# Attention and the layers behind it in one hand-ordered region: the drain of attention, the first in-blocks and their banks

## The chip, the cores and the metric

The kernel runs on one core of one Trainium2 chip. What is measured is the device time of one execution in microseconds (us). A core has TensorE (PE, matmuls, whose weight loads the profile lists as PEld), VectorE (DVE), ScalarE (ACT), GpSimd (POOL) and SyncE (SP, which issues most of the transfers). Each engine runs its own list of instructions in order and waits on semaphores for the others. PSUM, into which PE writes, has eight banks.

## What is computed

Windowed attention with four sink keys over q, k, v of shape (2, 8, 768, 64), then two feed-forward layers of 512 to 2048 to 512 over the 1536 tokens:

```python
scores = scale * np.matmul(q, k.transpose(0, 1, 3, 2))
keep = is_sink | in_window                      # 4 sinks, window of 128
scores = np.where(keep, scores, -1000000000.0)
a = np.exp(scores - max); a = a / (sum + 1e-09)
x = np.matmul(a, v)                             # to (1536, 512)
h = np.maximum(x @ w_in, 0.0);  x = h * h @ w_out            # layer 1
h = x @ w_in2; g = h * np.tanh(log1p(exp(h))); out = g @ w_out2   # layer 2
```

## The kernel before

**Attention** works on 12 tiles of 128 query rows and in each on 4 pairs of heads, 48 pairs in all. A loop over pair steps n (from -3 to 52) is software-pipelined: at step n it issues the scores of pair n+4 (`emit_s`, tile `s`), the exp of pair n+3 (`emit_exp`, on ScalarE), the normalization of pairs n+2, n+3 (`emit_norm`, on POOL, at even n), the transposes of pairs n-1, n (`emit_t`, tile `pt`, at odd n), their copies to SBUF (`evac_t`, tile `pts`, on ScalarE or DVE) and the products with v of pairs n-4, n-3 (`emit_av`, tile `av`, at even n). When a tile of rows is done, `emit_x` copies it out (`xf`, on ScalarE), casts it to a rounded part `xh` (POOL) and subtracts to get the rest `xl`: on POOL for the first ten tiles, and for tiles 10 and 11 on DVE, one or more steps later (`split_x`). Once the scores run out, at step 44, the last steps are the drain. PSUM is split into four banks for `s`, three for `pt` and one for `av`, in this order.

**A layer** works on 3 groups of 512 tokens (`xh[0]` to `xh[2]`; tiles 8 to 11 are group 2) and on 16 blocks of 128 hidden units. A sub-step n is one group and one block: an in-block of 12 matmuls into a bank `h`, then relu, square and a cast to `gh` on ScalarE (`relu_squared`), a subtraction to `gl` on DVE (`low_part`), and one sub-step later the out-block: 12 matmuls into four accumulators `o`, in the order gh·wol, gl·woh, gh·woh for each. PSUM has four banks for `h` and four for `o`.

**Weights** come as 64-bit words (tile `raw`, three slots) and each block's two halves, wi and wo, are converted by a `Conv`: a scaled copy of the high words (`head`, ScalarE), two DVE instructions on the bits (`mid_r`, lines 136 and 142), one that joins them (`mid_or`, line 148), the rounded part on ScalarE (`high`: wih or woh, line 167) and the rest on DVE (`low`: wil or wol, line 171). Three of them (`blocks` 0 to 2: block 0's wi and wo, block 1's wi) are done during attention, at the pair steps that the table `PLAN` gives; the function `slot` does the others in layer 1, two to each sub-step, those that `done_w` doesn't name, in the order wi(2), wo(1), wi(3), wo(2) and on. `IN_AT` gives the pair steps at which attention issues the in-blocks of sub-steps 0 and 1; they lie in banks of `s`, and their relu and gl follow one and two steps later.

The loop over pairs and the layers stand in two regions (`tc.manual_schedule()`), each with the order of its code. Across the two, the built program has the layers' first conversions in between the drain's last instructions.

Of the kernel before, what the change touches and what calls it, by code (L numbers as in the profile page):

```python
# [9 lines left out]
F32 = mybir.dt.float32  # L10
# [5 lines left out]
ALU = mybir.AluOpType  # L16
PSUM = bass.MemoryType.PSUM
P = 128
# [5 lines left out]
def f32(ap):  # L24
    return ap.bitcast(F32)
# [3 lines left out]
def kernel(  # L29
# [13 lines left out]
    nc = tc.nc  # L43
# [3 lines left out]
    NB = S // P  # L47
    NPAIR = H // 2
# [143 lines left out]
    def in_products(ph, w, sp):  # L192
        for m, (a, x) in enumerate([("wil", xh[sp]), ("wih", xl[sp]), ("wih", xh[sp])]):
            for d in range(NDC):
                nc.tensor.matmul(  # L195
                    ph, lhsT=w[a][:, d, :], rhs=x[:, d, :],
                    start=(m == 0 and d == 0), stop=(m == 2 and d == NDC - 1),
                )

    def new_g(pool):  # L200
        return [pool.tile([P, TS], F32R, tag=nm, name=nm, bufs=2) for nm in ("gh", "gl")]

    def relu_squared(ph, gh):
        nc.scalar.activation(out=ph, in_=ph, func=AF.Relu)  # L204
        nc.scalar.activation(out=ph, in_=ph, func=AF.Square)
        nc.scalar.copy(gh, ph)  # L206

    def low_part(x, gh, gl):
        nc.vector.tensor_tensor(out=gl, in0=x, in1=f32(gh), op=ALU.subtract)  # L209


    att = ExitStack()
    apool = att.enter_context(tc.tile_pool(name="apool", bufs=1))
    ps_s = att.enter_context(tc.tile_pool(name="ps_s", bufs=4, space=PSUM, reuse_waits="tile"))
    ps_p = att.enter_context(tc.tile_pool(name="ps_p", bufs=3, space=PSUM, reuse_waits="tile"))
    ps_a = att.enter_context(tc.tile_pool(name="ps_a", bufs=1, space=PSUM, reuse_waits="tile"))

    tiles = [(b, i) for b in range(B) for i in range(NB)]
    qn, kn, vn = {}, {}, {}
# [100 lines left out]
    def prep(t, which, half=None):  # L320
        if t >= len(tiles):
            return
        b, i = tiles[t]
        js = slice(0, NPAIR) if half is None else slice(half * NPAIR // 2, (half + 1) * NPAIR // 2)
        src = (qn if which == "q" else kn)[b, i]
        pt = ps_p.tile([P, NPAIR, P], F32, tag="pt", name="tr")
        for j in range(js.start, js.stop):
            nc.tensor.transpose(  # L328
                pt[:, j, :], src[:, 2 * j : 2 * j + 2, :].rearrange("p h d -> p (h d)"), ident
            )  # L330
        if which == "q":
            nc.vector.tensor_copy(kt[:, js, qpos(t) : qpos(t) + P], pt[:, js])
        else:
            p0 = kpos(i)
            nc.scalar.copy(kt[:, js, p0 : p0 + P], pt[:, js])
# [164 lines left out]
    def emit_x(b, i):  # L500
        hi, lo = x_slot(b, i)
        x = apool.tile([P, NPAIR, P], F32, tag="xf", name="xf", bufs=1)
        nc.scalar.copy(x, av.pop((b, i)))
        nc.gpsimd.tensor_copy(hi, x)
        if b * NB + i < len(tiles) - 2:
            nc.gpsimd.tensor_tensor(out=lo, in0=x, in1=f32(hi), op=ALU.subtract)
        else:
            st["x"] = (x, hi, lo)

    def split_x():  # L510
        if "x" in st:
            x, hi, lo = st.pop("x")
            nc.vector.tensor_tensor(out=lo, in0=x, in1=f32(hi), op=ALU.subtract)

    blocks = []
    for fb in range(W1N):
        wt[0, fb] = weight_tiles(w1pool, fb)
        blocks += [Conv(conv, 0, fb, part, wt[0, fb]) for part in ("wi", "wo")]
    WARM = (6, 3, 2, 1)
    PLAN = {  # L520
        0: {5: "load", 11: "head", 14: "mid_r1", 18: "mid_r2", 22: "mid_or", 26: "high low"},
        2: {36: "load", 41: "head_pool", 44: "mid_r", 45: "mid_or", 46: "high low"},
        1: {37: "load", 46: "head mid_r", 47: "mid_or", 48: "high low"},
    }

    IN_AT = (46, 48)
    SINKS = {n0 + 2 * (i - 2): i for n0 in (-1, NB * NPAIR - 3) for i in range(2, NB)}
    early, ready = {}, {}
    NPR = len(pairs)
    with tc.manual_schedule():  # L530
        load_limits()
        nc.scalar.preload_act_table_set("natural_log_exp_and_others")
        load_tile(0, "qk", halves=2)
        load_tile(1, "qk")
        load_tile(2, "kq")
        load_tile(0, "v")
        load_tile(3, "kq")
        positions()
        load_tile(1, "v")
        load_tile(2, "v")  # L540
        load_rest(2)
        warm = apool.tile([P, P], F32, name="warm")
        nc.vector.memset(warm, 0.0)
        nc.vector.memset(one, 1.0)
        nc.gpsimd.memset(two, 2.0)
        for x in prs:
            nc.gpsimd.memset(x[:, :, WIN:], 0.0)
        for x in sums:
            nc.vector.memset(x, 1e-9)
        idle = ps_a.tile([P, P + 2], F32, tag="av", name="idle")  # L550

        def keep_warm(times):
            for _ in range(times):
                nc.tensor.matmul(idle[:, 0:P], lhsT=warm, rhs=warm, start=True, stop=True)  # L554

        keep_warm(WARM[0])
        limits(idle[:, P : P + 2])
        first_mask()
        prep(0, "q", 0)
        keep_warm(WARM[1])  # L560
        prep(0, "k", 0)
        keep_warm(WARM[2])
        emit_s(*pairs[0])
        emit_max(*pairs[0], 0)
        emit_max(*pairs[0], 1)
        prep(0, "q", 1)
        prep(0, "k", 1)
        emit_s(*pairs[1])
        emit_max(*pairs[1], 0)
        emit_max(*pairs[1], 1)  # L570
        second_mask()
        window_masks()
        emit_exp(*pairs[0])
        for n in range(-3, NPR + 5):
            at = {d: pairs[n + d] for d in range(-4, 5) if 0 <= n + d < NPR}
            last = {d for d in at if at[d][2] == NPAIR - 1}
            t, j = divmod(n, NPAIR)
            if n % 2 and 0 in at:
                emit_t([at[-1], at[0]])
            if 4 in at and n > -3:  # L580
                emit_s(*at[4])
            if 3 in at and n > -3:
                emit_exp(*at[3])
            if 4 in at and n > -3:
                emit_max(*at[4], 0)
            if 4 in at and n > -3:
                emit_max(*at[4], 1)
            if n % 2 == 0:
                split_x()
                group = [at[d] for d in (2, 3) if d in at]  # L590
                if group:
                    emit_rs(group)
                for p in group:
                    emit_norm(*p)
            if -4 in last:
                emit_x(*at[-4][:2])

            if n % 2 == 0:
                if n >= 0 and j == 2:
                    prep_rows(t + 2)  # L600
                for d in (-4, -3):
                    if d in at:
                        emit_av(*at[d])
            for _ in range((1, 2, 0, 1)[j]):
                evac_t()
            if n in (-3, -2):
                prep(1, "qk"[n + 3])
            if n >= 0 and j == NPAIR - 1:
                load_tile(t + 4, "q", halves=1 + (t + 5 == len(tiles)))
                load_tile(t + 4, "k", halves=1 + (t + 6 >= len(tiles)))  # L610
                load_tile(t + 3, "v")
                load_rest(t + 3)
            if n in SINKS:
                sink_keys(SINKS[n])
            if n < 0:
                keep_warm(WARM[3])
            if n == 1:
                fast_flag()
            for fb in range(W1N):
                if n == IN_AT[fb]:  # L620
                    early[fb] = ps_s.tile([P, TS], F32, tag="s", name="h")
                    in_products(early[fb], wt[0, fb], 0)
                if n == IN_AT[fb] + 1:
                    ready[fb] = new_g(gpool)
                    relu_squared(early[fb], ready[fb][0])
                if n == IN_AT[fb] + 2:
                    low_part(early[fb], *ready[fb])
            for m, steps in PLAN.items():
                for step in steps.get(n, "").split():
                    getattr(blocks[m], step)()  # L630
    att.close()


# [261 lines left out]
    ps_o = mo.enter_context(tc.tile_pool(name="ps_o", bufs=4, space=PSUM, reuse_waits="tile"))  # L895
    engines = [getattr(mybir.EngineType, e) for e in ("PE", "DVE", "Activation", "Pool", "SP")]
    tc.mark_branch_hint_location("general", hint="LikelyTaken", engines=engines)
    with tc.manual_schedule():
        moe(
            wt, lambda fb: w1pool if fb < W1N else w2pool, conv, gpool, ps_h, ps_o,  # L900
            done_in=ready, done_w=[(0, blocks[m].fb, blocks[m].part) for m in PLAN],
        )
    mo.close()
    main.close()

# [141 lines left out]
```

## Time and profile before

| | |
|---|---|
| median of 3 runs | 614.54 us (614.17 to 614.92) |
| the profiled execution | 614.09 us, of which the trace's span is 612.3 us |
| PE, DVE, ScalarE, POOL busy | 98%, 74%, 57%, 12% of the span |
| matmuls of the layers start | 79.79 us (h of sub-step 0), 90.24 us (first out-block) |
| last matmul ends | 607.35 us |

A timeline row gives the start in us, the duration, the engine, the line, the operation with the tiles written and read, and the count; at its end may stand the idle time before it and what ended that. A row's duration includes the engine's latency, so back-to-back instructions start closer together than their durations say. Attention's drain is at 76 to 90 us; the conversions of layer 1's weights run on DVE and ScalarE until about 160 us.

### The profile page before, as it was taken

The numbers are of one execution on the slowest core, as the hardware profiler recorded it, in microseconds if no ns is written. First come the engines' busy times: TensorE is split into PE (matmuls) and PEld (weight loads), VectorE is DVE, ScalarE is ACT, GpSimd is POOL, SyncE is SP. The second block draws the span as 40 slices with busy tenths as digits, with TensorE's granted clock in tenths as the row PEclk, the third lists the DMA queues.
The fourth block names the chain that finished last, engine by engine and source line by source line (L and its number), as shares of the span: only waits on it lengthen the run. The fifth ranks groups of instructions, "written<-read, shape, count | busy, mean of one in ns | idle before, by whom it ended". The sixth has DMA issues, their size and how long they took to land.

```text
span 612.3 us, 10256 instructions
## 1 busy us (share of the span) xinstructions
PE 602.5 (98%) x3854; PEld 493.7 (81%) x3854; DVE 452.9 (74%) x951; ACT 349.6 (57%) x723; POOL 70.6 (12%) x103
## 2 busy tenths in 40 slices
PE   9999989999999999999999999999999999999996
PEld 6786778888888888888888888888888888888885
DVE  5898889989621111188889699999888778887784
ACT  4999976777643333277777555555454444544442
POOL 5889940000000000000000000000000000000000
PEclk9999999999999999999999999999999999999999
DMA  9989746666400000036666300000010000100001
GB/s 190 191 179 185 195 139 179 202 204 196 148 1 0 2 0 1 0 113 197 205 190 193 101 1 2 0 1 1 1 69 1 0 1 0 44 27 1 0 1 71
DMA packets 71704, 49.45 MB, mean 81 GB/s; under 512 B 49508, under 2 KB 66148, under 8 KB 71652
## 3 DMA queue, kind: packets, MB, share of 16 engines
q1 hardware_dynamic: 71360, 48.38, 29.1%
q8 instruction: 31, 0.51, 0.3%
q10 hardware_dynamic: 292, 0.39, 0.2%
q14 instruction: 21, 0.17, 0.1%
HBM read 45.61 MB, written 3.15 MB: 80 GB/s over the span
## 4 chain that ended last, share of the span: by engine, by line
PE 94%; DVE 2%; POOL 1%; ACT 1%; issue 1%; DVEq 0%; ACTq 0%; POOLq 0%
PE o L658 43%; PE h L195 42%; PE s L398 3%; PE av L488 3%; PE pt L451 2%; PE idle L554 1%; PE tr L346 1%; POOL pr L439 1%; DVE cv_r L142 0%; PE tr L328 0%; ACT pr L419 0%; DVE cv_a L148 0%; DVE pts L466 0%; DVE s L409 0%; DVE cv_r L136 0%
## 5 line engine op out<-in xcount | busy, mean ns | idle before, releaser
L195 PE MATMUL h<-xh,wil 128*128 128x512 f32 x384 | 102.9, 390 | 0.0
L195 PE MATMUL h<-xl,wih 128*128 128x512 f32 x384 | 102.6, 389 | 0.0
L195 PE MATMUL h<-xh,wih 128*128 128x512 f32 x384 | 102.6, 389 | 0.0
L209 DVE TENSOR_TENSOR gl<-h,gh 128x512 fp32r<-128x512 f32 x48 | 33.2, 691 | 89.7 <-ACT gh L206 89.7
L195 PEld LDWEIGHTS h<-xl,wih 128*128 128x128 f32 x384 | 72.1, 188 | 15.0
L195 PEld LDWEIGHTS h<-xh,wih 128*128 128x128 f32 x384 | 72.1, 188 | 15.0
L195 PEld LDWEIGHTS h<-xh,wil 128*128 128x128 f32 x384 | 71.9, 188 | 15.0
L658 PE MATMUL o<-gh,wol 128*128 128x512 f32 x192 | 74.8, 390 | 1.5 <-DVE wol L171 1.5
L726 ACT ACTIVATE e<-t,small 128x512 f32<-128x512 f32 x48 | 34.8, 725 | 70.4 <-DVE t L722 70.4
L658 PE MATMUL o<-gh,woh 128*128 128x512 f32 x192 | 74.7, 389 | 0.0
L658 PE MATMUL o<-gl,woh 128*128 128x512 f32 x192 | 74.7, 389 | 0.0
L204 ACT ACTIVATE h<-h 128x512 f32<-128x512 f32 x48 | 27.9, 582 | 77.9 <-PE h L195 77.9
L658 PE MATMUL o<-wol,gh 128*128 128x512 f32 x176 | 68.5, 389 | 0.0
L658 PE MATMUL o<-woh,gl 128*128 128x512 f32 x176 | 68.5, 389 | 0.0
L658 PE MATMUL o<-woh,gh 128*128 128x512 f32 x176 | 68.5, 389 | 0.0
L742 ACT CAST gh<-t 128x512 fp32r<-128x512 f32 x44 | 27.4, 623 | 46.4 <-PE o L658 43.0
L148 DVE SCALAR_TENSOR_TENSOR cv_a<-cv_a,cv_r 128x512 int32<-128x512 int32 x64 | 44.6, 697 | 6.2
L209 DVE TENSOR_TENSOR gl<-t,gh 128x512 fp32r<-128x512 f32 x44 | 30.3, 689 | 19.8 <-ACT gh L742 19.8
L419 ACT ACTIVATE pr<-s,nm 128x208 f32<-128x208 f32 (+2 forms) x96 | 40.5, 436 | 5.3 <-DVE nm L409 4.9
L439 POOL TENSOR_TENSOR pr<-pr,rs 128x416 f32<-128x416 f32 (+2 forms) x48 | 42.3, 902 | 9.5 <-DVE rs L431 6.3
L658 PEld LDWEIGHTS o<-gh,wol 128*128 128x128 f32 x192 | 36.0, 188 | 8.9 <-DVE wol L171 1.6
L128 ACT ACTIVATE cv_a<-raw 128x512 f32<-128x512 f32 x63 | 42.3, 673 | 0.2 <-DMA raw<-in_moe_w_in_dram 0.2
(107 smaller groups left out, 998.1 us busy)
## 6 DMA issues: line engine op xcount, KB each, us to landing
raw<-in_moe_w_in_dram SPq DMA_DIRECT2D x32, 512.0 KB, 4.0
raw<-in_moe_w_out_dram SPq DMA_DIRECT2D x32, 512.0 KB, 4.3
vn<-in_v_dram SPq DMA_DIRECT2D x12, 256.0 KB, 5.7
qn<-in_q_dram SPq DMA_DIRECT2D x10, 256.0 KB, 5.0
kn<-in_k_dram SPq DMA_DIRECT2D x9, 256.0 KB, 4.6
vx<-in_v_dram SPq DMA_DIRECT2D x16, 128.0 KB, 4.1
out_dram<-ob SPq DMA_DIRECT2D x8, 256.0 KB, 2.4
kn<-in_k_dram SPq DMA_DIRECT2D x6, 128.0 KB, 3.0
```

The costliest lines, as they stand in the source:

```text
L128: nc.scalar.activation(out=self.a, in_=high_words, func=AF.Copy, scale=2.0**-112)
L148: nc.vector.scalar_tensor_tensor(out=ai, in0=ai, scalar=3, in1=self.r, op0=ALU.logical_shift_left, op1=ALU.bitwise_or)
L195: nc.tensor.matmul(ph, lhsT=w[a][:, d, :], rhs=x[:, d, :], start=(m == 0 and d == 0), stop=(m == 2 and d == NDC - 1),)
L204: nc.scalar.activation(out=ph, in_=ph, func=AF.Relu)
L209: nc.vector.tensor_tensor(out=gl, in0=x, in1=f32(gh), op=ALU.subtract)
L398: nc.tensor.matmul(banks[e][qs, 0:w], lhsT=kt[r, j, q1], rhs=kt[r, j, k0 : k0 + w], start=True, stop=True, skip_group_check=True,)
L419: nc.scalar.activation(out=pr[b, i][:, 2 * j + e, 0:w], in_=banks[e][:, 0:w], func=AF.Exp, bias=nm[:, e : e + 1], scale=-1.0, accum_out=sm ...
L439: nc.gpsimd.tensor_tensor(out=x, in0=x, in1=rs.to_broadcast([P, 2, w]), op=ALU.mult)
L488: nc.tensor.matmul(av[b, i][e * D : (e + 1) * D, j, qs], lhsT=x[0:kv, 2 * j + e, :], rhs=pts[0:kv, c, e, qs], start=(j == 0 and m == 0), s ...
L658: nc.tensor.matmul(acc[sp][t], lhsT=a, rhs=x, start=(fb == 0 and m == 0), stop=(fb == NFB - 1 and m == 2),)
L726: nc.scalar.activation(out=e, in_=t, func=AF.Ln, bias=two)
L742: nc.scalar.copy(g_tiles(n)[0], et[n][1])
```

## The change

Both regions become one, so that every engine has the order of the code: first the whole loop over pairs, then the layers. Five conversions instead of three are done in attention (block 1's wo and block 2's wi are new) and their steps in `PLAN` move. The in-blocks of sub-steps 0 and 1 are issued at pair steps 44 and 49, at the head of the step, instead of 46 and 48 at its end; relu and cast follow in the same step, gl at steps 47 and 51. All xl are subtracted on POOL. One copy out of `pt` moves from step 47 to 48. The PSUM pool of `av` comes first, so that `h` of the layers lies over `av` and three banks of `s`, and `o` over the last bank of `s` and those of `pt`; two half transposes at the start take banks of `s`. Block 2's weights lie in the pool of blocks 0 and 1.

```diff
+    ps_a = att.enter_context(tc.tile_pool(name="ps_a", bufs=1, space=PSUM, reuse_waits="tile"))
     ps_s = att.enter_context(tc.tile_pool(name="ps_s", bufs=4, space=PSUM, reuse_waits="tile"))
     ps_p = att.enter_context(tc.tile_pool(name="ps_p", bufs=3, space=PSUM, reuse_waits="tile"))
-    ps_a = att.enter_context(tc.tile_pool(name="ps_a", bufs=1, space=PSUM, reuse_waits="tile"))
...
-        pt = ps_p.tile([P, NPAIR, P], F32, tag="pt", name="tr")
+        pool, tag = (ps_s, "s") if half == 0 else (ps_p, "pt")
+        pt = pool.tile([P, NPAIR, P], F32, tag=tag, name="tr")
...
         nc.gpsimd.tensor_copy(hi, x)
-        if b * NB + i < len(tiles) - 2:
-            nc.gpsimd.tensor_tensor(out=lo, in0=x, in1=f32(hi), op=ALU.subtract)
-        else:
-            st["x"] = (x, hi, lo)
+        nc.gpsimd.tensor_tensor(out=lo, in0=x, in1=f32(hi), op=ALU.subtract)
...
-    for fb in range(W1N):
+    for fb in range(W1N + 1):
         wt[0, fb] = weight_tiles(w1pool, fb)
...
-        2: {36: "load", 41: "head_pool", 44: "mid_r", 45: "mid_or", 46: "high low"},
+        2: {36: "load", 44: "head mid_r", 45: "mid_or", 47: "high low"},
...
+        3: {46: "load", 49: "head", 50: "mid_r", 51: "mid_or", 52: "high low"},
...
-    IN_AT = (46, 48)
+    IN_AT, LOW_AT = (44, 49), (47, 51)
...
-    with tc.manual_schedule():
+    order = ExitStack()
+    order.enter_context(tc.manual_schedule())
...
+            for fb in range(W1N):
+                if n == IN_AT[fb]:
+                    early[fb] = ps_s.tile([P, TS], F32, tag="s", name="h")
+                    in_products(early[fb], wt[0, fb], 0)
             if n % 2 and 0 in at:
                 emit_t([at[-1], at[0]])
...
             if n % 2 == 0:
-                split_x()
...
-            for _ in range((1, 2, 0, 1)[j]):
+            for _ in range((1, 2, 0, 1)[j] - (n == NPR - 1) + (n == NPR)):
                 evac_t()
...
+            for fb in range(W1N):
+                if n == IN_AT[fb]:
+                    ready[fb] = new_g(gpool)
+                    relu_squared(early[fb], ready[fb][0])
+                if n == LOW_AT[fb]:
+                    low_part(early[fb], *ready[fb])
...
-    with tc.manual_schedule():
-        moe(
-            wt, lambda fb: w1pool if fb < W1N else w2pool, conv, gpool, ps_h, ps_o,
...
+    moe(
+        wt, lambda fb: w1pool if fb <= W1N else w2pool, conv, gpool, ps_h, ps_o,
...
+    order.close()
```

**How the order moves.** PE at the start of the drain, from the last scores (`s`, pair 47) on. Before:

```order
L398 MATMUL s<-kt 64x208 x4
L488 MATMUL av<-pts,vn 64x64 x2
L488 MATMUL av<-pts,vx 64x64 x4
L488 MATMUL av<-pts,vn 64x64 x4
L488 MATMUL av<-pts,vx 64x64 x4
L488 MATMUL av<-pts,vn 64x64 x2
L451 MATMUL pt<-ident,pr_109 128x64 x16
L488 MATMUL av<-pts,vn 64x64 x2
```

With the change:

```order
L399 MATMUL s<-kt 64x208 x4
L195 MATMUL h<-xh_67,wil_111 128x512 x4
L195 MATMUL h<-xl_70,wih_110 128x512 x4
L195 MATMUL h<-xh_67,wih_110 128x512 x4
L489 MATMUL av<-pts,vn 64x64 x2
L489 MATMUL av<-pts,vx 64x64 x4
L489 MATMUL av<-pts,vn 64x64 x4
L489 MATMUL av<-pts,vx 64x64 x4
L489 MATMUL av<-pts,vn 64x64 x2
L452 MATMUL pt<-ident,pr_109 128x64 x16
```

The in-block of sub-step 0 (three rows `h`) stands right behind the last scores, ahead of two groups of `av` and one of transposes; before, it came behind both groups.

ScalarE from the relu of sub-step 1's in-block on (in the names the digit behind wih, woh, wil, wol is the block). Before:

```order
L204 ACTIVATE h_2041<-h_2041 128x512
L205 ACTIVATE h_2041<-h_2041 128x512
L206 CAST gh_2056<-h_2041 128x512
L503 COPY xf_2078<-av_2022 128x512
L167 CAST wih2_2121<-cv_a_2109 128x512
L128 ACTIVATE cv_a_2131<-raw_2107 128x512
```

With the change:

```order
L204 ACTIVATE h_2054<-h_2054 128x512
L205 ACTIVATE h_2054<-h_2054 128x512
L206 CAST gh_2073<-h_2054 128x512
L167 CAST wih2_118<-cv_a_2028 128x512
L504 COPY xf_2097<-av_2032 128x512
L167 CAST woh1_116<-cv_a_2070 128x512
```

wih of block 2 now stands behind this relu, square and cast directly and ahead of `xf`, and woh of block 1 behind that.

DVE from the wol of block 1 to the next gl, that of sub-step 2. Before:

```order
L171 TENSOR_TENSOR wol1_117<-cv_a_2115,woh1_116 128x512
L136 TENSOR_SCALAR cv_r_2140<-raw_2127 128x512
L142 TENSOR_SCALAR cv_r_2140<-raw_2127 128x512
L148 SCALAR_TENSOR_TENSOR cv_a_2139<-cv_a_2139,cv_r_2140 128x512
L171 TENSOR_TENSOR wil3_2162<-cv_a_2131,wih3_2161 128x512
L136 TENSOR_SCALAR cv_r_2172<-raw_2129 128x512
L142 TENSOR_SCALAR cv_r_2172<-raw_2129 128x512
L148 SCALAR_TENSOR_TENSOR cv_a_2171<-cv_a_2171,cv_r_2172 128x512
L171 TENSOR_TENSOR wol2_2124<-cv_a_2139,woh2_2123 128x512
L209 TENSOR_TENSOR gl_2189<-h_2175,gh_2188 128x512
```

With the change, from the same instruction on:

```order
L171 TENSOR_TENSOR wol1_117<-cv_a_2070,woh1_116 128x512
L136 TENSOR_SCALAR cv_r_2131<-raw_2124 128x512
L142 TENSOR_SCALAR cv_r_2131<-raw_2124 128x512
L148 SCALAR_TENSOR_TENSOR cv_a_2130<-cv_a_2130,cv_r_2131 128x512
L136 TENSOR_SCALAR cv_r_2137<-raw_2126 128x512
L142 TENSOR_SCALAR cv_r_2137<-raw_2126 128x512
L148 SCALAR_TENSOR_TENSOR cv_a_2136<-cv_a_2136,cv_r_2137 128x512
L171 TENSOR_TENSOR wil3_2143<-cv_a_2130,wih3_2142 128x512
L136 TENSOR_SCALAR cv_r_2153<-raw_2128 128x512
L142 TENSOR_SCALAR cv_r_2153<-raw_2128 128x512
L148 SCALAR_TENSOR_TENSOR cv_a_2152<-cv_a_2152,cv_r_2153 128x512
L171 TENSOR_TENSOR wol2_121<-cv_a_2136,woh2_120 128x512
```

and the rows that follow these:

```order
L136 TENSOR_SCALAR cv_r_2161<-raw_2148 128x512
L142 TENSOR_SCALAR cv_r_2161<-raw_2148 128x512
L148 SCALAR_TENSOR_TENSOR cv_a_2160<-cv_a_2160,cv_r_2161 128x512
L171 TENSOR_TENSOR wil4_2183<-cv_a_2152,wih4_2182 128x512
L136 TENSOR_SCALAR cv_r_2193<-raw_2150 128x512
L142 TENSOR_SCALAR cv_r_2193<-raw_2150 128x512
L148 SCALAR_TENSOR_TENSOR cv_a_2192<-cv_a_2192,cv_r_2193 128x512
L171 TENSOR_TENSOR wol3_2145<-cv_a_2160,woh3_2144 128x512
L209 TENSOR_TENSOR gl_2210<-h_2196,gh_2209 128x512
```

Between wol of block 1 and gl stood two conversions (L136, L142, L148), one wil and one wol; now there stand five conversions, two wil and two wol.

## Rows read from the trace of the kernel before

**Rows 1.** Table of windows: window, its us, each engine's busy us, PE clock, DMA.

```profile
76.09:90.24 14.15, 11.89 (x185) 9.65 (x185) 12.30 (x26) 10.15 (x22) 7.28 (x9) 1.00 0.37 122
90.24:101.25 11.01, 11.01 (x48) 9.11 (x49) 10.46 (x20) 7.35 (x14) 0.46 (x1) 1.00 0.59 179
101.25:160.00 58.75, 58.75 (x261) 48.65 (x260) 53.32 (x100) 43.87 (x77) 0.00 (x0) 1.00 0.66 197
160.00:607.35 447.35, 447.33 (x1974) 370.08 (x1972) 314.46 (x523) 224.30 (x377) 0.00 (x0) 1.00 0.13 42
```

**Rows 2.** Timeline of PE, 71.9 to 101.5 us.

```profile
71.92 0.71 PE L451 MATMUL pt<-ident,pr 64*128 64x64 f32 x16
...
75.51 0.58 PE L398 MATMUL s<-kt 64*64 64x208 f32 x8
76.43 0.34 PE L488 MATMUL av<-pts,vn 128*64 128x64 f32 x4 [0.34 <-ACT xf L503]
...
78.71 0.34 PE L488 MATMUL av<-pts,vn 128*64 128x64 f32 x4
...
79.79 1.20 PE L195 MATMUL h<-xh,wil 128*128 128x512 f32 x4
...
82.74 0.71 PE L451 MATMUL pt<-ident,pr 64*128 64x64 f32 x16
...
90.24 0.50 PE L658 MATMUL o<-gh,wol 128*128 128x512 f32 x1 [1.47 <-DVE wol L171]
...
93.09 1.07 PE L195 MATMUL h<-xh,wil 128*128 128x512 f32 x4
...
101.25 0.39 PE L658 MATMUL o<-gh,wol 128*128 128x512 f32 x1
101.48 0.39 PE L658 MATMUL o<-gl,woh 128*128 128x512 f32 x1
```

**Rows 3.** Timeline of DVE, layer 1's conversions and gl of sub-step 2.

```profile
93.57 0.69 DVE L171 TENSOR_TENSOR wol<-cv_a,woh 128x512 fp32r<-128x512 f32 x1
94.17 0.42 DVE L136 TENSOR_SCALAR cv_r<-raw 128x512 int32<-128x512 int32 x1
94.63 0.47 DVE L142 TENSOR_SCALAR cv_r<-raw 128x512 uint16<-128x512 uint32 x1
95.20 0.69 DVE L148 SCALAR_TENSOR_TENSOR cv_a<-cv_a,cv_r 128x512 int32<-128x512 int32 x1
95.81 0.69 DVE L171 TENSOR_TENSOR wil<-cv_a,wih 128x512 fp32r<-128x512 f32 x1
...
98.65 0.68 DVE L209 TENSOR_TENSOR gl<-h,gh 128x512 fp32r<-128x512 f32 x1
```

**Rows 4.** Timeline of ScalarE in the drain.

```profile
75.30 0.19 ACT L419 ACTIVATION_READ_ACCUMULATOR pr<-s,nm 128x1 f32 x1
...
87.72 0.58 ACT L204 ACTIVATE h<-h 128x512 f32<-128x512 f32 x1 [0.33 <-PE h L195]
...
89.43 0.59 ACT L503 COPY xf<-av 128x512 f32<-128x512 f32 x1
89.91 0.63 ACT L167 CAST wih<-cv_a 128x512 fp32r<-128x512 f32 x1
```

**Rows 5.** Timeline of POOL in the drain.

```profile
76.54 1.72 POOL L439 TENSOR_TENSOR pr<-pr,rs 128x416 f32<-128x416 f32 x2
...
78.90 1.34 POOL L506 TENSOR_TENSOR xl<-xf,xh 128x512 fp32r<-128x512 f32 x1
```

**Rows 6.** DMA issues, 60 to 112 us: tiles, queue, count, KB, median us to landing.

```profile
raw<-in_moe_w_in_dram SPq DMA_DIRECT2D x8, 512.0 KB, 4.4
```

**Rows 7.** Timeline of DVE, line 142 beside POOL's subtraction.

```profile
79.14 1.42 DVE L142 TENSOR_SCALAR cv_r<-raw 128x512 uint16<-128x512 uint32 x1
```

**Rows 8.** Table of windows behind the last matmul, columns as in rows 1.

```profile
610.00:611.00 1.00, 0.00 (x0) 0.00 (x0) 0.00 (x0) 0.00 (x0) 0.00 (x0) 0.74 0.03 8
611.00:612.30 1.30, 0.00 (x0) 0.00 (x0) 0.00 (x0) 0.00 (x0) 0.00 (x0) 0.50 0.00 0
```

More of the change, by code (lines that the diff above doesn't have):

```diff
@@ L504, in emit_x @@
         nc.gpsimd.tensor_copy(hi, x)
-        if b * NB + i < len(tiles) - 2:
-            nc.gpsimd.tensor_tensor(out=lo, in0=x, in1=f32(hi), op=ALU.subtract)
-        else:
-            st["x"] = (x, hi, lo)
[L510 to L513, printed above, removed]
+        nc.gpsimd.tensor_tensor(out=lo, in0=x, in1=f32(hi), op=ALU.subtract)
     blocks = []
-    for fb in range(W1N):
+    for fb in range(W1N + 1):
         wt[0, fb] = weight_tiles(w1pool, fb)
@@ L521 @@
         0: {5: "load", 11: "head", 14: "mid_r1", 18: "mid_r2", 22: "mid_or", 26: "high low"},
-        2: {36: "load", 41: "head_pool", 44: "mid_r", 45: "mid_or", 46: "high low"},
-        1: {37: "load", 46: "head mid_r", 47: "mid_or", 48: "high low"},
+        2: {36: "load", 44: "head mid_r", 45: "mid_or", 47: "high low"},
+        1: {37: "load", 44: "head", 45: "mid_r1", 46: "mid_r2", 48: "mid_or high", 49: "low"},
+        4: {38: "load", 47: "head", 48: "mid_r1", 49: "mid_r2 mid_or", 50: "high", 51: "low"},
+        3: {46: "load", 49: "head", 50: "mid_r", 51: "mid_or", 52: "high low"},
     }
-    IN_AT = (46, 48)
+    IN_AT, LOW_AT = (44, 49), (47, 51)
     SINKS = {n0 + 2 * (i - 2): i for n0 in (-1, NB * NPAIR - 3) for i in range(2, NB)}
@@ L529 @@
     NPR = len(pairs)
-    with tc.manual_schedule():
+    order = ExitStack()
+    order.enter_context(tc.manual_schedule())
+    if True:
         load_limits()
@@ L618 @@
                 fast_flag()
[L619 to L627, printed above, removed]
             for m, steps in PLAN.items():
@@ L897 @@
     tc.mark_branch_hint_location("general", hint="LikelyTaken", engines=engines)
-    with tc.manual_schedule():
-        moe(
-            wt, lambda fb: w1pool if fb < W1N else w2pool, conv, gpool, ps_h, ps_o,
-            done_in=ready, done_w=[(0, blocks[m].fb, blocks[m].part) for m in PLAN],
-        )
+    moe(
+        wt, lambda fb: w1pool if fb <= W1N else w2pool, conv, gpool, ps_h, ps_o,
+        done_in=ready, done_w=[(0, blocks[m].fb, blocks[m].part) for m in PLAN],
+    )
+    order.close()
     mo.close()
```

## The prediction

> **What bounds the kernel now.** I read the table of windows first. TensorE (PE) has a fixed amount of work, and from 90.24 us to its last matmul at 607.35 us it has no gap: busy 11.01 of 11.01 us, then 58.75 of 58.75, then 447.33 of 447.35 [rows 1]. So a microsecond gained or lost ahead of that stretch goes straight to the end of the kernel, unless a new gap opens inside it. The window just before, 76.09 to 90.24, is attention's drain: PE is busy 11.89 of 14.15 us, so 2.26 us are idle. That is all that reordering the drain can win.
>
> PE's timeline says where they are [rows 2]: 0.34 us before the av of pairs 40 and 41, which wait for ScalarE's xf, smaller gaps around the transposes, and 1.47 us before the first out-block, which waits for VectorE's (DVE) wol of block 0. I call the in-block of sub-step n h(n) and its out-block out(n). Both parts of g pass through ScalarE (gh) and then DVE (gl). The first matmul of out(2) that reads gl starts at 101.48 [rows 2]; DVE has finished gl(2) at 98.65 + 0.68 = 99.33 [rows 3]. That leaves 2.15 us of slack, the number on which this prediction turns.
>
> **The change, part by part.** *(a) h(0) at pair step 44.* Its bank is that of a score tile of pair 46, whose exp has been read by 75.30 + 0.19 = 75.49 [rows 4], so it starts when PE has done the last scores, at 75.51 + 0.58 = 76.09 [rows 2]. It takes 82.74 − 79.79 = 2.95 us, to 79.04, and covers the wait for xf. The av behind it takes 79.79 − 78.71 = 1.08 (four such groups stand in the drain), to 80.12, and the transposes of pairs 44 and 45 take 0.71, to 80.83. Their normalization on GpSimd (POOL) was done at 76.54 + 1.72 = 78.26 with a weight head in front of it [rows 5]; without the head it is done no later. Both early waits go.
>
> *(b) DVE up to wil(1).* DVE's copy of those transposes can start at 80.85. In unhindered issue intervals [rows 3], a subtraction, shift-or or copy takes 0.60, and a weight conversion (L136, L142, L148) 95.81 − 94.17 = 1.64, of which the first two are 0.46 and 0.57, or 0.46 both where nothing waits on them. Copy, shift-or, L136 and L142 bring DVE to 80.85 + 0.60 + 0.60 + 0.46 + 0.46 = 82.97. ScalarE's wih(1), behind the xf of tile 10, is ready at about 83.0. wil(1) then meets POOL's cast and subtraction for tile 10. I add 0.3 for that (bounds below) and have it done at 84.0; h(1) runs 84.0 to 86.95.
>
> *(c) Out(0).* av of the last two pairs ends at 86.95 + 1.08 = 88.03; wol(0) is done by about 87.1, gl(0) earlier. Out(0) starts at 88.05 against 90.24: **2.2 us earlier**. It takes 93.09 − 90.24 = 2.85, later blocks (101.25 − 93.09) / 3 = 2.72 each [rows 2]; so h(2) starts at 90.9, out(1) at 93.6, h(3) at 96.35, and h(3) ends at 99.06. wil(2) (90.0), wol(1) (92.3) and wil(3) (96.1) come in time.
>
> *(d) Where the stall goes.* ScalarE runs relu, square, cast and wih(2) behind h(1): the same four, with one copy of 0.48 between, took 87.72 to 90.53 [rows 4], so 2.33 without it. wih(2) lands at 86.98 + 2.33 = 89.3, just when DVE comes to it. wil(2), shift-or and gl(1) go to 91.1; woh(1) is ready at 91.2. **wol(1) starts** at 91.2, or 91.55 with 0.35 for POOL's subtraction of tile 11 beside it. Before it started at 93.57.
>
> Then comes what the pieces of DVE's order show. Before, wol(1) is followed by a conversion, wil, a conversion, wol, and gl(2): 98.65 − 93.57 = 5.08 us. In the change five conversions and wil(3), wol(2), wil(4), wol(3) stand between, since the blocks made in the drain pull every later block one sub-step forward, while gl(2) keeps its sub-step: 0.60 + 5 × 1.64 + 4 × 0.60 = 11.2 us. gl(2) starts at 91.55 + 11.2 = 102.75 and is done at 103.43, **4.1 us later** than before, with 2.15 us of slack to pay from. The gl-matmul of out(2) runs at 103.46 against 101.48.
>
> ScalarE's gh(2) is held up with it: its relu stands behind woh(3), which waits for the fourth of those conversions (99.9); woh 0.63, then 1.71 from relu to behind the cast's issue [rows 4], give about 102.4. So PE should idle from 99.06 to 102.4, run one matmul, and wait again to 103.46: 4.1 us in all.
>
> *(e) The rest.* The two subtractions leave DVE (counted by leaving them out) and cost POOL 1.3 us each; no matmul needs tiles 10 and 11 before the third token group. The half transposes at the start move to other banks, but the scores behind them wait for the same copies and exps: nothing. The weight loads use three slots on SyncE's queue; the shortest new round from freeing a slot to reading it again is 0.6 + 1.64 + 0.6 + 1.64 + 0.6 = 5.1 us against 4.4 to land [rows 6], so they stay hidden; a load of 5.5 us would add 0.4. From out(2) on a sub-step costs DVE 5.08 and PE 2 × 2.72 = 5.44, so there is no second stall, and nothing that gives time back.
>
> **Sum.** 103.46 − 101.48 = +2.0 us on the profiled execution's 614.09 us: 616.1. That execution lies 0.45 below the median of the three runs (614.54); I put the forecast between, at **616.3 us**.
>
> **Bounds of the unknown,** which is what POOL's work beside DVE costs. At one end nothing, and ScalarE never late: from DVE's copy at 80.85 it is 12 × 0.60 + 3 × 1.03 to the end of wol(1) and 10.6 more to gl(2): 101.7, done at 102.4, net +0.9. Below that no row reaches, if DVE keeps the order shown. At the other end, L142 at 79.14 took 1.42 us while POOL's subtraction ran from 78.90 to 80.24 [rows 5, 7], against 0.47 undisturbed [rows 3]. If wil(1) and wol(1) each lose such 0.95, the sum is 2.0 − 0.65 + 1.9 = +3.2. I took 0.65 for both, nearer the low end, since by this timing DVE comes to wil(1) ahead of POOL's subtraction. [...]
>
> **Rivals.** *1. The drain's gain survives (faster).* Place: gl(2). It decides at 99.3: if gl(2) is there when PE has done h(3), the 2.2 us stay, 611.9 to 612.3. For it: all that PE waited for in the drain is earlier. Against: the way from wol(1) to gl(2) would have to fit in 7.6 us, where the row intervals say 11.2. It needs an error in my reading of DVE's order. Chance 0.09.
>
> *2. Only a small loss.* DVE meets none of the waits, or runs its conversions closer together than the rows show; net −0.6 to +1.2, 613.9 to 615.5. For it: DVE was busy 12.30 of 14.15 us in the drain [rows 1], so it has idle time to use. Against: the gaps are waits that it shares with ScalarE. Chance 0.19.
>
> *3. The stall also lowers TensorE's clock.* [...] PE would stand idle 3.3 us, run one matmul, and stand 0.8. No row has a matmul at the lower level; if the clock falls, one sub-step of 5.2 us at half the rate adds 2.6, and half or twice that by how soon it rises: net +3.3 to +7, 617.5 to 621. [...] Chance 0.12.
>
> *4. The forecast,* net +1.2 to +3.3: 0.60.
>
> **How the numbers follow.** A measurement of this kernel tells 0.2% (1.2 us) from no change. Slower by more: 0.60 + 0.12 and a sliver of rival 2, 0.73. Within: nearly all of rival 2, 0.17. Faster by more: rival 1 and a sliver, 0.10. The range from 614.4 to 618.6 takes in the forecast with both bounds, much of rival 2 and the mild end of rival 3.
>
> **What would show it.** Right: h(0) near 76, no idle row above 0.3 us before the first out-block, out(0) near 88; then PE idle between about 99 and 103.5 behind ScalarE's gh (L206) and DVE's gl (L209), DVE at work without a pause, and no gap after. gl(2) done before 100 us makes the forecast wrong; a granted clock below 1.00 behind 102 us makes it rival 3; out(0) after 89 means that POOL's overlap or wih(1) costs more than I put in.

## The result, and the profile after

The changed kernel takes 618.93 us (median of 6 runs, 618.53 to 620.55), the kernel before in the same session 614.23 (6 runs, 613.99 to 614.92). The ratio is 1.0079, with a 95% interval from 1.0066 to 1.0093: **slower by 0.8%**. The profiled execution took 618.53 us with a span of 616.7, against 614.09 and 612.3 before: +4.4.

The table of windows of the changed kernel, cut at its own stages (columns as in [rows 1]: the window, its us, the busy us and instructions of PE, PEld, DVE, ScalarE and POOL, then PE's granted clock, the DMA share and GB/s):

```profile
75.90:87.97 12.07, 11.69 (x189) 9.56 (x185) 10.19 (x21) 9.35 (x20) 7.62 (x8) 1.00 0.28 88
87.97:99.28 11.31, 11.01 (x51) 8.80 (x48) 10.34 (x20) 6.45 (x12) 2.27 (x2) 1.00 0.67 195
99.28:104.02 4.74, 0.97 (x5) 0.24 (x3) 4.50 (x9) 4.15 (x8) 0.00 (x0) 1.00 0.78 226
104.02:111.00 6.98, 6.98 (x23) 5.55 (x24) 6.57 (x13) 4.96 (x9) 0.00 (x0) 0.76 0.69 211
111.00:160.00 49.00, 49.00 (x218) 40.59 (x217) 44.57 (x84) 36.43 (x64) 0.00 (x0) 1.00 0.65 198
160.00:611.64 451.64, 451.64 (x1993) 373.77 (x1991) 314.06 (x521) 225.41 (x379) 0.00 (x0) 1.00 0.13 41
```

The drain (first row) lost nearly all its idle time: 0.38 us against 2.26 in [rows 1]. Two rows are new in kind. From 99.28 to 104.02 PE does 0.97 us of work in 4.74. From 104.02 to 111.00 it is busy throughout, but the granted clock is 0.76 in the mean. From 111.00 on it is busy at 1.00 to the last matmul, which ends at 611.64 against 607.35: what was lost by 111.00, and only that, reaches the end.

PE's timeline has the same in single instructions (at the end of a row: idle time before it, and what ended that):

```profile
75.90 1.20 PE L195 MATMUL h<-xh,wil 128*128 128x512 f32 x4
...
83.90 1.21 PE L195 MATMUL h<-xh,wil 128*128 128x512 f32 x4 [0.29 <-DVE wil L171]
...
87.97 0.50 PE L655 MATMUL o<-gh,wol 128*128 128x512 f32 x1
...
96.72 1.20 PE L195 MATMUL h<-xh,wil 128*128 128x512 f32 x4 [0.30 <-DVE wil L171]
...
102.96 0.49 PE L655 MATMUL o<-gh,wol 128*128 128x512 f32 x1 [3.20 <-ACT gh L206]
104.02 0.50 PE L655 MATMUL o<-gl,woh 128*128 128x512 f32 x1 [0.57 <-DVE gl L209]
...
105.46 0.63 PE L655 MATMUL o<-gh,wol 128*128 128x512 f32 x1
...
111.00 0.39 PE L655 MATMUL o<-gh,wol 128*128 128x512 f32 x1
```

The first out-block starts at 87.97, 2.27 us earlier than the 90.24 of [rows 2]. Then PE waits 3.20 us for ScalarE's gh(2), runs one matmul, and waits 0.57 for DVE's gl(2). The second matmul of out(2) is at 104.02 against 101.48: **+2.54, the stall's net**. From there to the first matmul of out(3) it takes 111.00 − 104.02 = 6.98 us; before it was 106.69 − 101.48 = 5.21, by [rows 2] and this row of the same timeline of the kernel before:

```profile
106.69 0.39 PE L658 MATMUL o<-gh,wol 128*128 128x512 f32 x1
```

That is **+1.77, the clock**. Together 4.31 of the span's 4.4. The rows at half rate last 0.63 instead of 0.39 us each.

The clock by the microsecond (same columns):

```profile
103.00:104.00 1.00, 0.45 (x1) 0.14 (x1) 1.00 (x3) 0.98 (x2) 0.00 (x0) 1.00 0.80 168
104.00:105.00 1.00, 0.98 (x4) 0.85 (x5) 0.86 (x3) 0.56 (x1) 0.00 (x0) 1.00 0.89 328
105.00:106.00 1.00, 1.00 (x4) 0.76 (x4) 1.00 (x2) 0.48 (x2) 0.00 (x0) 0.53 0.26 102
106.00:107.00 1.00, 1.00 (x4) 0.81 (x3) 0.96 (x3) 0.97 (x3) 0.00 (x0) 0.50 0.70 151
107.00:108.00 1.00, 1.00 (x3) 0.73 (x3) 0.90 (x3) 0.97 (x3) 0.00 (x0) 0.50 0.95 338
108.00:109.00 1.00, 1.00 (x5) 0.80 (x4) 1.00 (x3) 1.00 (x2) 0.00 (x0) 0.77 0.97 163
```

The fall comes at about 105.1, one microsecond *after* PE has resumed work, and the lower level (0.50) holds to about 108.5, although PE is fully busy. Who reads only the waits does not find these 1.77 us: there is no idle row in them.

DVE's timeline tells why gl(2) is late:

```profile
86.33 0.69 DVE L171 TENSOR_TENSOR wol<-cv_a,woh 128x512 fp32r<-128x512 f32 x1 [0.35 <-ACT woh L167]
...
89.36 0.69 DVE L171 TENSOR_TENSOR wil<-cv_a,wih 128x512 fp32r<-128x512 f32 x1 [0.40 <-ACT wih L167]
89.97 1.10 DVE L148 SCALAR_TENSOR_TENSOR cv_a<-cv_a,cv_r 128x512 int32<-128x512 int32 x1
90.99 0.68 DVE L209 TENSOR_TENSOR gl<-h,gh 128x512 fp32r<-128x512 f32 x1
91.75 1.02 DVE L171 TENSOR_TENSOR wol<-cv_a,woh 128x512 fp32r<-128x512 f32 x1
92.70 0.42 DVE L136 TENSOR_SCALAR cv_r<-raw 128x512 int32<-128x512 int32 x1
...
102.68 0.68 DVE L171 TENSOR_TENSOR wol<-cv_a,woh 128x512 fp32r<-128x512 f32 x1
103.28 0.68 DVE L209 TENSOR_TENSOR gl<-h,gh 128x512 fp32r<-128x512 f32 x1
```

From 92.70 to 103.28 DVE works without a pause through five conversions, two wil and two wol. Nothing in that stretch waits; gl(2) simply stands last. POOL's timeline for the two long rows ahead of it:

```profile
89.88 0.64 POOL L505 CAST xh<-xf 128x512 fp32r<-128x512 f32 x1 [4.89 <-ACT xf L504]
90.60 1.62 POOL L506 TENSOR_TENSOR xl<-xf,xh 128x512 fp32r<-128x512 f32 x1
```

L148 lies beside the cast and takes 1.10 us, wol(1) beside the subtraction and takes 1.02; undisturbed both are 0.69 [rows 3]. Each ends 0.55 us behind the POOL instruction that it met (L148 at 91.07 behind 90.52, wol(1) at 92.77 behind 92.22), while gl(1), which reads h from PSUM, starts in the middle of the subtraction and takes its usual 0.68. In these two rows, 0.55 us of an instruction that takes 0.69 undisturbed lies behind the end of POOL's.

And ScalarE, from woh(3), the row ahead of the relu, to gh(2):

```profile
100.57 0.62 ACT L167 CAST woh<-cv_a 128x512 fp32r<-128x512 f32 x1 [0.22 <-DVE cv_a L148]
101.09 0.58 ACT L204 ACTIVATE h<-h 128x512 f32<-128x512 f32 x1
101.70 0.58 ACT L205 ACTIVATE h<-h 128x512 f32<-128x512 f32 x1
102.32 0.59 ACT L206 CAST gh<-h 128x512 fp32r<-128x512 f32 x1
```

The relu of h(2), whose matmuls ended near 93.5, starts at 101.09, behind woh(3), which waits for the L148 of the fourth conversion. The 3.20 us that the waits put down to gh are DVE's queue too.

### The profile page after: what moved, and what is told of

Its sections match the earlier page's. It is cut to its first block, busy times and chain, and to the rows that moved or that the text cites. A ratio compares the mean times of both kernels' runs of the same rounds, so it can differ in the third digit from the quotient of the medians.

```text
span 616.7 us, 10243 instructions
## 1 busy us (share of the span) xinstructions
PE 604.6 (98%) x3854; PEld 494.6 (80%) x3854; DVE 452.6 (73%) x949; ACT 350.6 (57%) x724; POOL 72.1 (12%) x104
## 4 chain that ended last, share of the span: by engine, by line
PE 93%; DVE 3%; POOL 2%; ACT 1%; issue 1%; DVEq 0%; ACTq 0%; POOLq 0%
PE o L655 42%; PE h L195 42%; PE s L399 3%; PE av L489 3%; PE pt L452 2%; POOL pr L440 1%; PE idle L551 1%; PE tr L347 1%; DVE cv_a L148 1%; DVE wil L171 0%; PE tr L329 0%; DVE cv_r L142 0%; DVE wol L171 0%; ACT pr L420 0%; DVE cv_r L136 0%
## 5 line engine op out<-in xcount | busy, mean ns | idle before, releaser
L148 DVE SCALAR_TENSOR_TENSOR cv_a<-cv_a,cv_r 128x512 int32<-128x512 int32 x64 | 44.9, 702 | 6.2
```

Of the source, the lines that this page charges most:

```text
L148: nc.vector.scalar_tensor_tensor(out=ai, in0=ai, scalar=3, in1=self.r, op0=ALU.logical_shift_left, op1=ALU.bitwise_or)
```

## The experiments

My theory after the result: all the loss is in out(2). Conversions pulled forward stand ahead of gl(2) on DVE (and, through woh, ahead of gh(2) on ScalarE), and the idle time then lowers the clock. The rivals: POOL's new work beside DVE makes gl(2) late, or the clock falls for another reason than idle time. Each run is set against runs of the kernel before on the same chip (614.17 us for the first four, 614.31 for the rest).

**1. Conversions back by one sub-step.** The drain stays as changed; the conversions of the layers return to the sub-steps that they had.

```diff
-            conv_at[m // 2 - (0 if done_w else AHEAD)].append(key)
+            conv_at[m // 2 + (1 if done_w else -AHEAD)].append(key)
```

> The changed kernel, with the layers' conversions put back one sub-step (wi(3) and wo(2) to sub-step 1, as before the change); nothing else differs. Theory (gl of sub-step 2 stands behind five conversions instead of two, and the stall, clock and all, comes from that alone): gl(2) starts 3 conversions' and 2 subtractions' worth less late, at about 91.75 + 0.95 + 3 x 1.64 + 2 x 0.60 = 98.8 us, out(2) at about 99.2 without a wait, no window with a granted clock below 1.00, and the kernel keeps the 2.2 us that the drain won: about 612.0 us, 0.3 to 0.4% faster than before. Rival A (the new banks or POOL's subtractions cost PE time by themselves): PE still waits over 1 us between 97 and 105 us, 614 us or more. Rival B (the clock falls for another reason than the stall, such as the different drain): no stall but a clock of 0.5 for some us, about 614 us.

Measured: 612.78 us (11 runs, 611.86 to 614.2), ratio 0.9976 (0.9967 to 0.9985), span 611.0, clock 1.00 in every window from 76 to 160 us. PE's waits from 75 us on (us in total, times, longest) are down to one group:

```profile
PE h L195 <- DVE wil L171: 0.6, 2, 0.3
```

DVE's timeline has gl(2) 4.6 us earlier than in the changed kernel:

```profile
89.87 1.10 DVE L148 SCALAR_TENSOR_TENSOR cv_a<-cv_a,cv_r 128x512 int32<-128x512 int32 x1
...
91.66 1.01 DVE L171 TENSOR_TENSOR wol<-cv_a,woh 128x512 fp32r<-128x512 f32 x1
...
98.70 0.69 DVE L209 TENSOR_TENSOR gl<-h,gh 128x512 fp32r<-128x512 f32 x1
```

Both rows beside POOL are as long as in the changed kernel, and the stall is gone, so POOL's work is not its cause. One line turns 0.8% slower into 0.24% faster than before: this is the best of the kernels here. It falls 0.8 us short of the 612.0 that I had expected: PE's last matmul ends 1.8 us earlier than before (605.53 against 607.35), not 2.4 as the first out-block does, since h(3) waits for wil(3) (0.27 us in its row, 0.57 by the start of out(2)), and the span is only 1.3 shorter, as 5.5 us instead of 5.0 lie behind the last matmul.

**2. Idle time filled.** The changed kernel with 13 matmuls of no use (their result is not read) ahead of out(2).

```diff
+            if l == 0 and n == 3 and done_w:
+                fill = ps_h.tile([P, TS], F32, tag="h", name="fill")
+                for k in range(13):
+                    nc.tensor.matmul(
+                        fill, lhsT=wt[0, 0]["wih"][:, k % 4, :], rhs=xh[0][:, k % 4, :], start=True, stop=True
+                    )
```

> The changed kernel with 13 more matmuls of 512 columns (13 x 0.227 = 2.95 us) on TensorE ahead of out(2), into a bank that nobody reads; they fit into the 3.2 us in which it waits for gh(2). Everything else waits as before, so gl(2) still comes at 104.0. Theory (idle time lowers the clock, and the fall costs 1.8 us of the 4.4): granted clock 1.00 throughout and a time 1.8 us below the changed kernel's, about 617.1 us. Rival (the fall has another cause, or it costs little): the clock still shows 0.5 behind 105 us and the time stays at 618.5 to 619.5 us.

Measured: 616.83 us (5 runs, 616.48 to 617.18), ratio 1.0041 (1.0028 to 1.0054). PE's timeline:

```profile
99.52 3.11 PE L863 MATMUL fill<-xh,wih 128*128 128x512 f32 x13
102.87 0.50 PE L655 MATMUL o<-gh,wol 128*128 128x512 f32 x1 [0.24 <-ACT gh L206]
103.94 0.50 PE L655 MATMUL o<-gl,woh 128*128 128x512 f32 x1 [0.57 <-DVE gl L209]
```

gl(2) is no earlier, the second matmul of out(2) is where it was (103.94 against 104.02), and yet the kernel is 2.1 us faster between the medians and 1.7 between the spans (615.0 against 616.7), with the clock at 1.00 in each microsecond from 99 to 108. So the fall is a cost of its own behind the stall, and it did not come where most of PE's idle time was filled (waits of 0.24 + 0.57 us, against 3.20 + 0.57 in the changed kernel).

**3. The two subtractions back on DVE.** Experiment 1, with xl of tiles 10 and 11 on DVE as before (in `split_x`, called at even pair steps).

> As the run with the conversions put back, and the subtractions xl of row tiles 10 and 11 on DVE again (at pair steps 48 and 52, as before the change) instead of POOL. Theory (POOL's subtraction blocks DVE's two-input instructions beside it): the joining shift-or and wol(1), which took 1.10 and 1.02 us beside POOL's xl, go back to 0.69, DVE pays 2 x 0.60 for the subtractions, and gl(2) comes 0.3 to 0.6 us later than with the conversions put back alone; h(3) may wait up to 0.5 us for wil(3): 612.0 to 612.8 us. Rival (no blocking; the long rows have another cause): the rows stay near 1.0 us and gl(2) comes 1.2 us later, 613 us.

Measured: 613.6 us (11 runs, 612.59 to 614.31), ratio 0.9991 (0.9982 to 1.0000), above the 612.0 to 612.8 that I had expected. DVE's timeline:

```profile
90.57 1.10 DVE L148 SCALAR_TENSOR_TENSOR cv_a<-cv_a,cv_r 128x512 int32<-128x512 int32 x1
...
92.19 0.68 DVE L514 TENSOR_TENSOR xl<-xf,xh 128x512 fp32r<-128x512 f32 x1
92.79 0.68 DVE L171 TENSOR_TENSOR wol<-cv_a,woh 128x512 fp32r<-128x512 f32 x1
...
99.50 0.68 DVE L209 TENSOR_TENSOR gl<-h,gh 128x512 fp32r<-128x512 f32 x1
```

wol(1) is back at 0.68, so POOL's subtraction had held it; L148 is at 1.10 still, beside the cast, which stays on POOL. But the subtraction now stands in DVE's queue, gl(2) comes 0.8 us later than in experiment 1, and h(3) waits 0.75 us for wil(3). By the profiles POOL is the better place for it; the medians say so by 0.8 us, with intervals that just overlap.

**4. One region alone.** The kernel before, with nothing changed but that both regions are one.

```diff
-    with tc.manual_schedule():
+    order = ExitStack()
+    order.enter_context(tc.manual_schedule())
+    if True:
...
-    with tc.manual_schedule():
-        moe(
...
+    moe(
...
+    order.close()
```

> The kernel before, with nothing changed but that both regions are one, so that each engine has the order of the code; steps, banks and conversions as before. Theory (the old order drew the layers' first conversions into DVE's gaps in the drain; in code order they come behind it): out(0) starts 1 to 2 us earlier, since wol(0) no longer has wi(2)'s conversion ahead of it, but h(2) then waits for wil(2), which is made only after gl(1) and wo(1)'s conversion: a wait of about 3.2 us before h(2), out(3) 1.8 us later than before, 616 us, and 2 us more if TensorE's clock falls. Rival (one region changes nothing by itself): 614.2 us within 0.3.

Measured: 616.66 us (6 runs, 615.89 to 619.13), ratio 1.0048 (1.0031 to 1.0065). PE's timeline:

```profile
88.00 0.50 PE L660 MATMUL o<-gh,wol 128*128 128x512 f32 x1
...
94.64 1.19 PE L195 MATMUL h<-xh,wil 128*128 128x512 f32 x4 [2.91 <-DVE wil L171]
```

One region alone makes the first out-block early too (88.00), and pays at h(2): the first conversions of the layers stand behind the whole drain on DVE, and PE waits 2.91 us for wil(2). So the early out-block needs the first conversions of the layers done ahead of it. The change did them in attention, and moved all the later conversions up as well.

**5. One half of a block earlier.** Experiment 1, with wi of block 3 alone in sub-step 0, to take away h(3)'s wait of 0.27 us.

```diff
+            conv_at[(m + 1) // 2 if done_w else m // 2 - AHEAD].append(key)
```

> This is the changed kernel with the layer conversions regrouped: the wi half of block 3 alone in sub-step 0, then wo of block 2 with wi of block 4, and so on, against two per sub-step from sub-step 1 on in the first experiment. Theory (DVE's order behind the drain is all that counts): wil(3) is ready before PE comes to h(3), so the 0.27-us wait there goes, gl(2) stays ahead of PE (below 99.5 us), no clock fall; about 612.5, 0.3 below the first experiment, which this measurement may not tell apart. Rival (any conversion ahead of gl(1) or gl(2) costs as much as it saves): the 0.3 come back at out(1) or out(2), 612.8 or above.

Measured: 616.1 us (6 runs, 615.01 to 617.82), ratio 1.0037 (1.0022 to 1.0051). I had expected a gain; it is a miss. I had reckoned with wil(3) alone, and the new pairs put wil(4) and a fourth conversion ahead of gl(2). DVE's timeline:

```profile
100.84 0.68 DVE L171 TENSOR_TENSOR wil<-cv_a,wih 128x512 fp32r<-128x512 f32 x1
101.44 0.68 DVE L209 TENSOR_TENSOR gl<-h,gh 128x512 fp32r<-128x512 f32 x1
```

And PE's at the same place:

```profile
101.11 0.50 PE L655 MATMUL o<-gh,wol 128*128 128x512 f32 x1 [2.35 <-ACT gh L206]
102.18 0.50 PE L655 MATMUL o<-gl,woh 128*128 128x512 f32 x1 [0.56 <-DVE gl L209]
```

Without meaning to, this run gave the point between. With three conversions between wol(1) and gl(2) (experiment 1) the second matmul of out(2) is at 99.68, with four at 102.18 (0.69 us of it a wait of DVE for wih(3)), with five (the change) at 104.02. gl(2)'s place in DVE's queue sets the time.

**6 and 7. Less fill.** Experiment 2 with 6 and with 10 matmuls instead of 13.

> The changed kernel with 6 instead of 13 unused matmuls of 512 columns ahead of out(2), about 1.3 us of work of no use in the 3.2-us wait. Theory (the fall of the clock follows from how long PE stands idle in total before 104 us): the wait ahead of out(2) shrinks to about 1.9 us and gl(2) is no earlier, so the stall as seen at the second matmul of out(2) stays at about 104.0. If 1.9 + 0.6 us of idle time are short enough, the clock stays at 1.00 and the median is that of the full fill, about 616.8; if not, the clock falls as in the changed kernel and the median is about 618.9. Rival (the fall is set by the place, by the load there, or by the second wait of 0.57 us alone): the clock falls as before, 618.9.

> The changed kernel with 10 unused matmuls of 512 columns ahead of out(2), between the 6 that left the clock fall as it was (1.87 us of waiting, then 0.57) and the 13 that did away with it (0.24, then 0.57). The first wait should be 1.87 - 4 x 0.23 = about 0.95 us, and the second matmul of out(2) again at about 104. Theory (a stretch with less waiting than some amount keeps the clock): no fall or a fall in few of the runs, 616.8 and a profile at 1.00. Rival (the second wait and the place decide, and only work right up to it helps): the fall is still there in most runs, 618.5 or more.

Measured: 618.89 us with 6 (5 runs, 618.08 to 619.3; ratio 1.0073, 1.0060 to 1.0086), 617.8 with 10 (6 runs, 616.77 to 619.91; 1.0061, 1.0044 to 1.0079). The first wait shrank to 1.87 and to 0.96 us, the second stayed at 0.57, and the profiled execution showed the fall in both. Windows of the run with 10:

```profile
104.00:105.00 1.00, 1.00 (x5) 0.77 (x4) 0.90 (x2) 0.46 (x1) 0.00 (x0) 0.62 0.37 131
105.00:106.00 1.00, 1.00 (x4) 0.81 (x3) 1.00 (x3) 0.77 (x2) 0.00 (x0) 0.50 0.33 85
106.00:107.00 1.00, 1.00 (x4) 0.81 (x3) 0.86 (x3) 0.94 (x3) 0.00 (x0) 0.50 0.87 278
```

With 6 the fall stayed, which both sides allowed, so this run does not tell them apart; with 10 neither side was right: three executions took 616.8 to 617.4 us at a mean clock of 0.998 to 1.000, and three 618.2 to 619.9 at 0.994 to 0.997. The lower level lasts 3.4 us in each of the three traces that show it (105.1 to 108.5 in the changed kernel, 104.8 to 108.2 with 6, 104.2 to 107.7 with 10, worked out from the granted clock of each microsecond). Less waiting made the fall rarer in these few executions, not shorter.

**8. The first in-block late.** Experiment 1 with h(0) at pair step 46.

```diff
-    IN_AT, LOW_AT = (44, 49), (47, 51)
+    IN_AT, LOW_AT = (46, 49), (48, 51)
```

> The first experiment with the in-block of sub-step 0 at pair step 46 instead of 44, with its relu and cast there and its gl at step 48. Theory (h of sub-step 0 covers the waits at the start of the drain): the av group behind the last scores waits 0.3 us for xf again and the transposes of pairs 44 and 45 some 0.3 for POOL, out(0) starts 0.3 to 0.7 later than 87.9; since wil(1) is what h(1) waits for and DVE starts its copy earlier without h(0) ahead of the transposes, part of it may be won back; 612.8 to 613.5. Rival (the place of h of sub-step 0 is worth nothing, the new weights in the drain are what makes out(0) early): 612.8, the time of the first experiment.

Measured: 613.47 us (11 runs, 612.87 to 614.39), ratio 0.9987 (0.9979 to 0.9996), span 612.0 against 611.0. PE's timeline:

```profile
76.50 0.34 PE L489 MATMUL av<-pts,vn 128*64 128x64 f32 x4 [0.34 <-ACT xf L504]
...
83.69 0.34 PE L489 MATMUL av<-pts,vn 128*64 128x64 f32 x4 [0.73 <-ACT xf L504]
...
88.97 0.50 PE L655 MATMUL o<-gh,wol 128*128 128x512 f32 x1
```

Two waits for xf come back, 1.07 us together, and out(0) starts at 88.97 instead of 87.87. The early h(0) is worth 1.0 us in the profiles, 0.7 in the medians, whose intervals just overlap.

## Why the prediction was wrong

- *(a) to (c), the drain: right.* h(0) at 75.90 (forecast 76.09), h(1) at 83.90 (84.0), out(0) at 87.97 (88.05). By the profile of experiment 8 the early h(0) is 1.1 us of it. One item was wrong: wil(3) did not come in time, and PE waited 0.30 us for it at 96.72. That does not reach the sum, because gl(2) decides when out(2) goes on.
- *(d), the stall: right place and mechanism, size short.* The part that I had counted, five conversions and four subtractions, came out as counted: 92.70 to 103.28 is 10.58 us (10.6). What was too small is the stretch before. wol(1) started at 91.75, not 91.55, and took 0.95 us to the next start, not 0.60: its end was set by the end of POOL's subtraction, at 92.22. Hence 104.02 instead of 103.46, and +2.54 instead of +2.0. For tile 11 I had priced POOL's subtraction once, at 0.35, ahead of wol(1), and its cast, which lengthened L148 by 0.41, not at all. The upper bound, +3.2, held it.
- *POOL beside DVE.* The rows of L148 and wol(1) show two DVE instructions with two inputs held up by a cast and by a subtraction (1.10 and 1.02 us against 0.69); for tile 11 I had counted the subtraction alone. The 1.42-us row, from which I took the upper bound, is no case of two inputs: L142 reads one tensor. That wil(1) would lose little because DVE comes to it ahead of POOL's subtraction was an estimate. It did start ahead (82.95 against 83.38), but beside the cast (82.47 to 83.30), and took 0.89 us. So it lost 0.20 and wol(1) 0.33, neither of them the 0.95 of the upper bound.
- *Rival 3: the step that failed.* The sum held the granted clock at 1.00 through the stall, that is, it put the clock at nothing. "The stall also lowers TensorE's clock", with a chance of 0.12, is what happened: the profiled execution shows 0.50 from 105.1 to 108.5 us, and the other five executions took as long or longer (618.53 to 620.55). My argument against it was that no row of before had a matmul at the lower level. The kernel before did pass its gap of 1.47 us with the clock at 1.00 [rows 1, 2], but that says nothing of a stretch with 0.97 us of work in 4.74. And [rows 8] spoke for the rival: a clock of 0.74 from 610 to 611 puts the fall about 3.1 us behind the last matmul, while my own (d) had PE idle for 3.3 us, then for 0.8 more. These rows gave no ground for a chance as low as 0.12. The price of the rival was fair: 2.6 for the clock against 1.77 in the profile and 2.1 between the medians. Its half rate was an estimate from the 0.50 of [rows 8], where no matmul runs, and no run shows that rate over a whole sub-step of 5.2 us: the changed kernel had 0.50 for 3.4 us.
- *(e), the rest: right.* No gap from 104.02 to the last matmul, and nothing that gave time back. ScalarE did wait for two loads (1.51 us before 98.22, 0.26 before 99.67), but DVE never stood behind it.

So two terms were short: the stall by 0.5 us, and the clock, which the sum did not hold, by about 2. With a clock that stayed, the forecast of 616.3 would have been 0.5 off: experiment 2, the same stall without the fall, measured 616.83.

## What to carry to other kernels

When work is pulled forward in an in-order queue, look for the one instruction that was *not* pulled forward with it and count what now stands ahead of it: here gl(2) kept its sub-step while each conversion moved up one, and the 2.27 us won in the drain were lost twice. A gap of a few microseconds on TensorE should be priced with the clock in mind: a fall costs here some 1.8 to 2.1 us more, in rows that show no wait. And before a rewrite is given up, try its parts: the drain as changed with the old conversion times is 0.24% faster than the kernel before.

## What was not expected of the hardware

Whether the clock falls behind the same stall seems to differ between executions of one kernel. Only the profiled execution of each kernel shows a fall in its rows. The last column counts executions with the longer time and a mean clock of 0.994 to 0.997; this is inferred, for the mean clock alone does not tell: executions of the kernel before show 0.996 and 0.997 too, at 613.8 to 615.1 us.

| kernel | waits of PE ahead of the resumed work, us | fall in the profiled execution | counted as fallen |
|---|---|---|---|
| the change | 3.20 + 0.57 | yes | 6 of 6 |
| experiment 5 | 2.35 + 0.56 | no | 3 of 6 |
| experiment 4 | 2.91 | no | 2 of 6 |
| experiment 6 (6 matmuls) | 1.87 + 0.57 | yes | 4 of 5 (the fifth: 618.08 us at 0.999) |
| experiment 7 (10 matmuls) | 0.96 + 0.57 | yes | 3 of 6 |
| experiment 2 (13 matmuls) | 0.24 + 0.57 | no | 0 of 5 |

So few executions do not tell 4 of 5 after 2.44 us of waits from 2 of 6 after 2.91; what decides stays open. The profiled executions alone show that it is not the length of the waits alone: rows at half rate followed 0.96 + 0.57 us, and none followed 2.91 or 2.35 + 0.56. The end of the kernels varies as well: behind the last matmul the granted clock falls after 2.0 us in the changed kernel and after 3.1 in the kernel before. That a fall can follow a stretch whose longest gap is 0.96 us is what I would have thought least likely.
